# A linear-attention layer and an MLP on one core: transposing DMAs joined two by two, two more groups transposed by DMA, and w_in issued at the start

## The chip, the core and the metric

The kernel runs on one core of one Trainium2 chip, in one launch. The metric is the device time of that launch in microseconds (us), as the median of several runs; lower is better. Engines are named as the profile names them: PE (TensorE matmul; PEld is its weight load), DVE (VectorE), ACT (ScalarE), POOL (GpSimd), SP (the engine that here only issues DMAs). "SPq" is SP's queue.

## The reference, cut to what matters

Four batches, eight heads, 768 time steps, head size 48. Each head carries a 48 x 48 state that decays by w and takes in the outer product of k and v; the output of a step also takes the current outer product weighted by u. The result, as 3072 tokens of 384 numbers, goes through an MLP with 2048 hidden units and a smooth ReLU. Inputs and output are float32.

```python
for t in range(S):
    cur = einsum('bhd,bhe->bhde', u[None] * kt, vt)
    y[:, :, t] = einsum('bhd,bhde->bhe', rt, state + cur)
    state = w[None, :, :, None] * state + einsum('bhd,bhe->bhde', kt, vt)
x = y.transpose(0, 2, 1, 3).reshape(B * S, H * D)
h = x @ w_in
g = where(h >= 1, h, where(h <= -1, 0, (h + 1) ** 2 / 4))
out = g @ w_out
```

## The kernel before, in words

Time is cut into 6 chunks of 128 steps. A unit is one batch in one chunk; a group is two units (256 tokens). There are 12 groups, 0 to 11; groups 0 and 1 are the first chunk of the four batches, 2 and 3 the second, and so on.

For each group, the rows of R, K and V are loaded by SP (L364, L438; 384 KB each; group 0's R and K come in halves, one a unit). V is cast to bf16 by ACT (L248, tile V from VF). Then come four products over the whole group: Rs = R times powers of the decay (Wup, L383), Ks = K times inverse powers (Wdn, L385), KU = K times u (L387), RKU = R times KU (L389). In groups 0 to 2 each product is given to POOL or DVE, later ones are on POOL alone. DVE sums RKU over the head (diag, L411), and diag times V is the current step's term (V2, shown as tile V, L416).

For each unit, R and K must be turned so that the head dimension lies on the partitions. In groups 0 to 4 (`g < TDMA`) PE does it: 8 transposes (T, L462), copied to SBUF by ACT or DVE (TT, L248). In groups 5 to 11 SP issues two transposing DMAs a group (RT from Rs, KT from Ks, L546). Then PE computes A (L473), DVE masks it (AT, L478), PE computes the chunk's contribution to the state (Sp, L485) and the output Y (from the carried state L495, from AT L500), DVE adds V2 (y, L507). The state is updated by DVE (Tm, L515) and POOL (state, L520) and cast by ACT (state_bf). y is turned by PE in groups 0 to 2 (X, L528, copied as xT) and from group 3 on by a transposing DMA for each unit (xT, L569).

The MLP of a group runs in 4 steps q of 512 hidden units. Each step is 12 matmuls (hp, L602), relu(0.5 h + 0.5) (pt, L610) and its square (sq, L615) on ACT, and min and max on DVE (gt, L620). The second layer takes 4 matmuls a unit and step (op, L651; 32 a group); the result is copied (o_sb) and stored by SP (out, L666). Group 0's first layer is done in pieces of half a step and a unit at a time. Row tiles have 3 buffers for R, 3 for K and 2 for V in float32.

The weights are loaded by POOL's own DMAs with a cast to bf16: w_in in four parts (L320), w_out in four parts (L326). Ahead of the first part of each, POOL copies one number of a row tile (`gone`, L314), so that the DMA waits until that load has landed: R of group 0, unit 1, for w_in, and K of group 1 for w_out.

What sets the order: nothing is ordered by hand. Every step is entered as an operation with its engine or engines, a planned cost, a key and the steps that it needs. A planner at the end of the function takes, time after time, the operation of the smallest key among those that can start next on that engine, and writes it out. Each engine then runs its instructions in that order. The tables TUNE (added to the keys, by kind of operation and group) and ONLY (which engine, where there are two) come from a search. Where the planner sees PE idle in the early part, it fills in matmuls on an identity (warm, L679), whose result nobody uses.

SP, too, issues in this order: a transposing DMA that waits for Ks or y holds back every load and store behind it.

Of the kernel before, what the change touches and what calls it, by code (L numbers as in the profile page):

```python
# [15 lines left out]
P = 128  # L16
# [7 lines left out]
def kernel(  # L24
# [86 lines left out]
    Rs = [const.tile([P, UNITS * H, HP], BF16, name="Rs", tag=f"Rs{i}") for i in range(NB)]  # L111
    Ks = [const.tile([P, UNITS * H, HP], BF16, name="Ks", tag=f"Ks{i}") for i in range(NB)]
    for i in range(NB):
        nc.vector.memset(Rs[i][:, :, D:], 0.0)
        nc.vector.memset(Ks[i][:, :, D:], 0.0)
# [31 lines left out]
    FLEX, XDMA, TDMA, VCAST = 3, 3, 5, 12  # L147

    def shift(what, g):
# [17 lines left out]
        'Wdn': {0: -9.14},  # L167
        'Wup': {0: 1.93},
        'X': {0: 0.79, 1: -2.24, 2: -4.04},
        'Y': {0: -0.05, 3: 3.62, 10: 0.23, 11: -1.39, 'm': -2.74},  # L170
        'decay': {2: 0.48, 3: -11.42, 'm': -2.78},
        'exps': {0: 7.52},
        'gate': {0: 20.08, 1: 8.66, 2: -1.81, 3: -14.22, 10: 0.46, 'm': -3.69},
        'load': {0: -2.22, 1: 2.92, 2: 1.11, 11: 5.77, 'm': 11.7},
        'lw': {0: 3.06},
        'lw_row': {0: -3.75},
# [6 lines left out]
        'u_bc': {0: 6.26},  # L183
        'u_row': {'m': -2.41},
        'usum': {0: -0.67, 1: 19.78, 2: 1.23, 3: -1.67, 10: -0.52, 11: 1.53, 'm': -1.65},
        'wCm': {0: 9.26},
        'w_in': {0: -0.2, 1: -1.68, 2: -0.05, 3: 2.64},
        'w_in!': {0: -5.6, 1: 36.74, 2: 2.76, 3: -7.13},
        'w_out': {0: 0.06, 1: -8.78, 2: 4.51, 3: -1.32},
        'w_out!': {1: -0.28, 2: -2.83, 3: 4.56},  # L190
        'w_power': {0: 0.75},
        'w_row': {0: 3.3},
        'w_take': {0: 5.37},
        'wc': {0: 5.72},
        'xT': {0: 9.53, 1: -3.07, 2: 0.34, 3: -1.67, 10: 0.36, 11: 5.32, 'm': -2.7},
        'y': {0: -3.24, 1: 0.72, 2: 1.77, 3: -1.94, 10: -14.8, 11: 4.13, 'm': -3.61},
    }
    ONLY = {
        'KU': {2: 1},
        'Ks': {0: 1, 1: 1},  # L200
        'RKU': {1: 0},
        'Rs': {0: 0},
        'TT': {0: 0, 1: 0, 2: 1},
        'V2': {0: 0, 1: 0, 2: 0},
        'o': {0: 0, 1: 1, 2: 0, 3: 0},
        'xT': {0: 0, 1: 0, 2: 0},
# [87 lines left out]
    op("w_row", (("NET", 0.0, 3.4),), -99, None)  # L294
    op("u_row4", (("NET", 0.0, 4.4),), -99, None)
    op("lw_row", (("ACT", 0.52, 0.05),), -98, lw_ln, ["w_row"])
    op("lw", (("PE", 1.3, 0.17),), -98, lw_mm, ["lw_row"], [("bank", "lw")], ["lw"])
    op("wc", (("PE", 0.6, 0.17),), -99, w_mm, ["w_row"], [("bank", "wc")], ["wc"])
# [4 lines left out]
    op("w_take", (("DVE", 0.15, 0.08),), -95, w_take, ["wc"], [], ["wc"])  # L303
# [5 lines left out]
    GATE_IN = {0: ("R", 0, 1)}  # L309
    GATE_OUT = {0: ("K", 1, 1)}  # L310
    for i in range(max(NW, NO)):
# [25 lines left out]
        op(f"w_in{i}!", (("POOL", 0.78 + 0.2 * (i in GATE_IN), 1.5),), k_in, w_in_go, after(GATE_IN, i, "w_in"), [], [GATE_IN[i][:2]] if i in GATE_IN else [])  # L337
        op(f"w_in{i}", (("SWD", 2.5, 1.35),), k_in, None, [f"w_in{i}!"])
        op(f"w_out{i}!", (("POOL", 0.78 + 0.2 * (i in GATE_OUT), 1.5),), k_out, w_out_go, after(GATE_OUT, i, "w_out"), [], [GATE_OUT[i][:2]] if i in GATE_OUT else [])
        op(f"w_out{i}", (("SWD", 10.6 / NO, 1.35),), k_out, None, [f"w_out{i}!"])  # L340

    def turned(n, i, p):
        g, j = divmod(n, UNITS)
# [461 lines left out]
```

## Time and profile before

| What | Value |
|---|---|
| median of 3 runs | 183.79 us (183.52 to 184.97) |
| the profiled execution | 183.7 us |
| its span, first to last instruction | 181.9 us |
| busy: PE, DVE, ACT, POOL | 171.7, 140.2, 133.8, 111.6 us |
| filler matmuls (L679) | 182, busy 14.6 us |
| transposing DMAs | 18 xT, 7 RT, 7 KT |
| DMA traffic | 27.75 MB, mean 153 GB/s |
| first relu (group 0) | at 18.77 us |
| first w_in DMA, first w_out DMA issued | at 6.34 and 20.26 us |

How to read it: the page lists busy times, slices of the span, DMA queues, the chain of work that ended last and the costliest groups of instructions. Times of the chain and of the timeline count from the start of the span. A line of a group reads: line, engine, operation, output<-input, shape, count, busy us and mean ns, idle time ahead of it and what ended that. The pattern "x4" is a count. GB/s counts the bytes as written, so a weight that is cast on the way counts half of what is read.

### The profile page before, as it was taken

The numbers are of one execution on the slowest core, as the hardware profiler recorded it, in microseconds if no ns is written. First come the engines' busy times: TensorE is split into PE (matmuls) and PEld (weight loads), VectorE is DVE, ScalarE is ACT, GpSimd is POOL, SyncE is SP. The second block draws the span as 40 slices with busy tenths as digits, with TensorE's granted clock in tenths as the row PEclk, the third lists the DMA queues.
The fourth block names the chain that finished last, engine by engine and source line by source line (L and its number), as shares of the span: only waits on it lengthen the run. The fifth ranks groups of instructions, "written<-read, shape, count | busy, mean of one in ns | idle before, by whom it ended". The sixth has DMA issues, their size and how long they took to land.

```text
span 181.9 us, 4539 instructions
## 1 busy us (share of the span) xinstructions
PE 171.7 (94%) x1850; PEld 129.7 (71%) x1850; DVE 140.2 (77%) x207; ACT 133.8 (74%) x169; POOL 111.6 (61%) x88
## 2 busy tenths in 40 slices
PE   5999999969999999999998999999899999999992
PEld 4897888747778787587876677767667777777761
DVE  6977499599998879789986888768687998754360
ACT  5455896678767978668986987786977798774762
POOL 2793553029999998979939949898859551000000
PEclk9999999999999999999999999999999999999999
DMA  6999999999997599998989999889798822101032
GB/s 123 189 214 188 212 199 186 176 208 182 193 192 162 96 218 196 141 215 180 147 151 168 178 200 183 162 179 206 142 183 108 193 83 65 22 4 43 0 130 86
DMA packets 103806, 27.75 MB, mean 153 GB/s; under 512 B 97125, under 2 KB 103786, under 8 KB 103786
## 3 DMA queue, kind: packets, MB, share of 16 engines
q1 hardware_dynamic: 100064, 24.32, 75.5%
q0 software_dynamic: 3712, 3.15, 10.7%
q8 instruction: 14, 0.23, 0.6%
q14 instruction: 6, 0.05, 0.1%
q10 hardware_dynamic: 10, 0.01, 0.0%
HBM read 20.45 MB, written 4.72 MB: 138 GB/s over the span
## 4 chain that ended last, share of the span: by engine, by line
PE 41%; DMA 17%; POOL 14%; SPq 13%; DVE 7%; issue 3%; ACT 3%; DVEq 0%; ACTq 0%; POOLq 0%
PE op L651 18%; PE hp L602 17%; DMA K<-in_k_dram 14%; SPq L364 8%; POOL RKU L389 4%; POOL state L520 3%; DVE gt L620 3%; POOL Ks L385 3%; SPq L438 3%; POOL KU L387 3%; DMA R<-in_r_dram 3%; PE A L473 2%; ACT sq L615 2%; SPq L546 1%; PE T L462 1%
## 5 line engine op out<-in xcount | busy, mean ns | idle before, releaser
L620 DVE SCALAR_TENSOR_TENSOR gt<-sq,hp 128x1024 bf16<-128x1024 f32 (+1 forms) x52 | 58.7, 1134 | 25.5 <-ACT sq L615 25.1
L602 PE MATMUL hp<-xT,w_in_sb 128*128 128x256 bf16 (+1 forms) x624 | 71.7, 264 | 1.8 <-DVE gt L620 1.0
L651 PE MATMUL op<-w_out_sb,gt 128*128 128x384 bf16 x384 | 72.3, 326 | 0.1
L602 PEld LDWEIGHTS <-w_in_sb 128*128 128x128 bf16 x624 | 57.1, 98 | 14.1 <-issue 3.4
L610 ACT ACTIVATE pt<-hp 128x1024 f32<-128x1024 f32 (+1 forms) x52 | 49.6, 954 | 23.5 <-PE hp L602 23.4
L615 ACT ACTIVATE sq<-pt 128x1024 f32<-128x1024 f32 (+1 forms) x52 | 51.6, 992 | 1.1
L651 PEld LDWEIGHTS <-gt 128*128 128x128 bf16 x384 | 34.6, 97 | 18.7 <-DVE gt L620 0.4
L478 DVE TENSOR_TENSOR AT<-A,umask 128x512 bf16<-128x512 f32 x48 | 30.9, 682 | 3.7 <-PE A L473 3.7
L416 POOL TENSOR_TENSOR V<-V,diag 128x768 f32<-128x768 bf16 (+1 forms) x13 | 17.9, 1378 | 16.9 <-DVE diag L411 13.7
L383 POOL TENSOR_TENSOR Rs<-R,Wup 128x768 bf16<-128x768 f32 (+1 forms) x12 | 20.4, 1702 | 5.3 <-DMA R<-in_r_dram 5.0
L520 POOL TENSOR_TENSOR state<-Tm,wCm 128x384 f32<-128x384 f32 x16 | 16.0, 1004 | 5.3 <-DVE Tm L515 5.1
L389 POOL TENSOR_TENSOR RKU<-R,KU 128x768 f32<-128x768 f32 x10 | 18.1, 1819 | 1.4 <-DVE KU L387 1.2
L385 POOL TENSOR_TENSOR Ks<-K,Wdn 128x768 bf16<-128x768 f32 x9 | 16.4, 1825 | 0.9 <-PE hp L602 0.5
L387 POOL TENSOR_TENSOR KU<-K,u_bc 128x768 f32<-128x768 f32 x9 | 16.4, 1828 | 0.0
L679 PE MATMUL warm<-ident 128*128 128x128 bf16 x182 | 14.6, 242 | 1.5 <-POOL ident masks.py:199 1.5
L679 PEld LDWEIGHTS <-ident 128*128 128x128 bf16 x182 | 12.8, 110 | 2.8 <-POOL ident masks.py:199 1.5
L507 DVE TENSOR_TENSOR y<-Y,V 128x384 bf16<-128x384 f32 x24 | 13.1, 551 | 0.8 <-issue 0.2
L248 ACT CAST state_bf<-state 128x384 bf16<-128x384 f32 x20 | 9.8, 506 | 5.1 <-POOL state L520 3.9
L500 PE MATMUL Y<-V,AT 128*128 128x48 bf16 x192 | 11.4, 183 | 1.1 <-ACT V L248 0.9
L248 ACT CAST V<-VF 128x768 bf16<-128x768 f32 x12 | 9.9, 828 | 3.2 <-DMA VF<-in_v_dram 3.1
L411 DVE TENSOR_REDUCE diag<-RKU 128x16 f32<-128x768 f32 (+1 forms) x13 | 11.3, 881 | 1.0 <-POOL RKU L389 1.0
L248 ACT COPY o_sb<-op 128x384 f32<-128x384 f32 x16 | 7.6, 474 | 5.8 <-PE op L651 5.8
(63 smaller groups left out, 127.4 us busy)
## 6 DMA issues: line engine op xcount, KB each, us to landing
VF<-in_v_dram SPq DMA_DIRECT2D x12, 384.0 KB, 5.5
out_dram<-o_sb SPq DMA_DIRECT2D x24, 192.0 KB, 2.3
R<-in_r_dram SPq DMA_DIRECT2D x11, 384.0 KB, 4.6
K<-in_k_dram SPq DMA_DIRECT2D x11, 384.0 KB, 6.0
w_in_sb<-in_moe_w_in_dram POOLq DMA_DIRECT2D x4, 384.0 KB, 9.3
w_out_sb<-in_moe_w_out_dram POOLq DMA_DIRECT2D x4, 384.0 KB, 9.2
R<-in_r_dram SPq DMA_DIRECT2D x2, 192.0 KB, 3.4
K<-in_k_dram SPq DMA_DIRECT2D x2, 192.0 KB, 3.8
```

The source lines that it names most:

```text
L248: nc.scalar.copy(out, in_) if e == "ACT" else engines[e].tensor_copy(out, in_)
L385: engines[e].tensor_mul(part(K_s)[:, :, :, :D], part(K), rep(Wdn, j1 - j0))
L387: engines[e].tensor_mul(part(tiles["KU", g]), part(K), rep(u_row, j1 - j0))
L389: engines[e].tensor_mul(part(tiles["RKU", g]), part(R), part(tiles["KU", g]))
L478: nc.vector.tensor_mul(tiles["AT", n][:, i], tiles["A", n][i], umask.unsqueeze(1).to_broadcast([P, NP, P]))
L520: nc.gpsimd.tensor_mul(states[b], tiles.pop(("Tm", n)), wCm)
L602: nc.tensor.matmul(hp[:, f - f0, cols], w_in_sb[:, i, n0 : n0 + P], tiles["xT", g][:, i, cols], start=(i == 0), stop=(i == nK - 1), skip_g ...
L610: nc.scalar.activation(tiles["pt", g, q][:, f0:f1], tiles["hp", g, q, x], AF.Relu, bias=0.5, scale=0.5)
L615: nc.scalar.activation(tiles["sq", g, q][:, f0:f1], tiles["pt", g, q][:, f0:f1], AF.Square, bias=0.0)
L620: nc.vector.scalar_tensor_tensor(out=tiles["gt", g, q][:, f0:f1], in0=tiles["sq", g, q][:, f0:f1], scalar=1.0, in1=tiles["hp", g, q, x], o ...
L651: nc.tensor.matmul(tiles["op", g, j], tiles["gt", g, q][:, f, j * P : (j + 1) * P], w_out_sb[:, n, :], start=(n == 0), stop=(n == nF - 1),)
L679: nc.tensor.matmul(tiles["warm"][:, :P], ident, ident, start=True, stop=True, skip_group_check=True)
```

## The change

- The two tiles Rs and Ks become one, RKs. From group 3 on (`TDMA` is 3 instead of 5) one transposing DMA a group turns both R and K of both units (RKT, 16 blocks of 128 x 128 instead of two times 8). Groups 3 and 4 thus lose their PE transposes (4 units) and the TT copies.
- y of both units lies in one tile, and from group 3 on one transposing DMA turns both (xT, 6 blocks instead of two times 3). xT is laid out by unit, then by block.
- `GATE_IN` is empty: POOL issues w_in without waiting for a row load. In the order that comes out, three parts come right behind the mask, the fourth behind the seven small products of w_power, which are now on POOL.
- Planned costs of some operations are changed, and with them and new TUNE and ONLY tables the planner writes out another order on all engines. In it, group 0's KU and RKU are on POOL and its Rs and Ks on DVE; group 1's Rs, Ks and KU are on DVE and its RKU on POOL; group 2's Rs, KU and Ks are on POOL (Rs, KU, Ks were on DVE) and its RKU and V2 on DVE. The last part of w_out is issued behind Rs of group 2. The filler matmuls become 141, of which 63 stand between A of group 0 and its Sp and Y.

The diff, cut to its core (line numbers in the program's list above are those of the kernel before):

```diff
-    Rs = [const.tile([P, UNITS * H, HP], BF16, name="Rs", tag=f"Rs{i}") for i in range(NB)]
-    Ks = [const.tile([P, UNITS * H, HP], BF16, name="Ks", tag=f"Ks{i}") for i in range(NB)]
+    RKs = [const.tile([P, 2, UNITS * H, HP], BF16, name="RKs", tag=f"RKs{i}") for i in range(NB)]
...
-    FLEX, XDMA, TDMA, VCAST = 3, 3, 5, 12
+    FLEX, XDMA, TDMA, VCAST = 3, 3, 3, 12
...
     ONLY = {
-        'KU': {2: 1},
-        'Ks': {0: 1, 1: 1},
-        'RKU': {1: 0},
-        'Rs': {0: 0},
-        'TT': {0: 0, 1: 0, 2: 1},
-        'V2': {0: 0, 1: 0, 2: 0},
+        'KU': {0: 0, 2: 0},
+        'Ks': {2: 0},
+        'RKU': {0: 0, 1: 0, 2: 1},
+        'Rs': {2: 0},
+        'TT': {1: 0, 2: 1},
+        'V2': {0: 0, 1: 0},
...
-    GATE_IN = {0: ("R", 0, 1)}
+    GATE_IN = {}
...
-                y = tiles["y", n] = att.tile([P, DM], BF16, name="y", tag="y", bufs=3)
+                if j == 0:
+                    tiles["y", g] = att.tile([P, UNITS, DM], BF16, name="y", tag="y", bufs=2)
...
-                    for i in range(2):
-                        def t_dma(e, g=g, i=i):
-                            t = tiles["RK"[i] + "T", g] = att.tile([P, UNITS * NP, P], BF16, name="RK"[i] + "T", tag="RK"[i] + "T", bufs=2)
-                            nc.sync.dma_start_transpose(out=t, in_=tiles["scaled", g][i].rearrange("p h d -> p (h d)"))
...
-                        op(f"{'RK'[i]}T{g}", (("DMA", 1.4, 3.0),), ka - 2 + i, t_dma, [f"{w_}{part}"] + ([f"RT{g}"] if i else []),
+                    def t_dma(e, g=g):
+                        t = tiles["RKT", g] = att.tile([P, 2 * UNITS * NP, P], BF16, name="RKT", tag="RKT", bufs=2)
+                        nc.sync.dma_start_transpose(out=t, in_=RKs[g % NB].rearrange("p i h d -> p (i h d)"))
+
+                    op(f"RKT{g}", (("DMA", 1.9, 2.7),), ka - 1.5, t_dma, [f"Rs{part}", f"Ks{part}"],
+                       [("RKT", ("RKT", g))], [("RKT", g), ("Rs", g), ("Ks", g)])
...
-                nc.sync.dma_start_transpose(out=tiles["xT", g][:, :, j * P : (j + 1) * P], in_=tiles["y", n])
+                tiles["xT", g] = moe.tile([P, UNITS, nK, P], BF16, name="xT", tag="xT", bufs=3)
+                nc.sync.dma_start_transpose(
+                    out=tiles["xT", g].rearrange("p u k t -> p (u k) t"), in_=tiles["y", g].rearrange("p u c -> p (u c)")
+                )
...
-                op(f"xT{n}", (("DMA", 1.2, 2.0),), ka + 3, x_dma, [f"y{n}"], [] if j else [("xT", ("xT", g))], [("y", n), ("xT", g)])
+            elif j == UNITS - 1:
+                op(f"xT{n}", (("DMA", 1.36, 1.6),), ka + 3, x_dma, [f"y{n - y}" for y in range(UNITS)], [("xT", ("xT", g))], [("y", g), ("xT", g)])
...
-                fill(int((spare - 0.1) / (0.11 if s < 7 else 0.06)))
+                fill(int((spare - 0.25) / (0.1 if s < 10 else 0.075)))
```

The tables TUNE, most planned costs and the times at which the planner lets each engine begin are changed as well and not shown.

More of the change, by code (lines that the diff above doesn't have):

```diff
@@ L185 @@
[L185 to L195, printed above, removed]
@@ new lines @@
+        'lw': {0: 1.04},
+        'lw_row': {0: -1.56},
[8 rows of a table added]
+        'wCm': {0: 0.97},
+        'w_in': {0: -1.94, 1: 0.83, 2: 1.91},
+        'w_in!': {0: 1.1, 1: 9.21, 2: 2.99, 3: 0.5},
+        'w_out': {0: -0.94, 1: -13.99, 2: -2.85, 3: -0.92},
+        'w_out!': {0: -1.21, 1: -0.54, 2: 2.86, 3: 1.24},
+        'w_power': {0: 1.68},
+        'w_row': {0: 7.69},
+        'w_take': {0: -1.25},
+        'wc': {0: 3.84},
+        'xT': {0: -2.42, 1: -3.58, 2: -3.06, 3: -4.14, 10: -0.73, 11: -6.46, 'm': -1.35},
@@ L207 @@
+        'o': {0: 0, 1: 1, 10: 1, 11: 0},
+        'w_power': {0: 0},
+        'xT': {2: 1},
     }
@@ L336 @@
         k_out = -1 + i * 0.1 + shift("w_out", i)
[L337 to L340, printed above, removed]
+        op(f"w_in{i}!", (("POOL", 0.78 + 0.6 * (i in GATE_IN), 2.5),), k_in, w_in_go, after(GATE_IN, i, "w_in"), [], [GATE_IN[i][:2]] if i in GATE_IN else [])
+        op(f"w_in{i}", (("SWD", 2.5, 0.6),), k_in, None, [f"w_in{i}!"])
+        op(f"w_out{i}!", (("POOL", 0.78 + 0.5 * (i in GATE_OUT), 2.5),), k_out, w_out_go, after(GATE_OUT, i, "w_out"), [], [GATE_OUT[i][:2]] if i in GATE_OUT else [])
+        op(f"w_out{i}", (("SWD", 10.6 / NO, 0.6),), k_out, None, [f"w_out{i}!"])
     def turned(n, i, p):
@@ L669 @@
             op(f"o {o}", where, k2 + 0.2 + shift("o", g), o_out, [f"mm2 {o}{nQ - 1}"], [("o_sb", ("o_sb", o))], [("op", o), ("o_sb", o)])
-            op(f"out {o}", (("DMA", 0.45, 2.0),), k2 + 0.3, store, [f"o {o}"], [], [("o_sb", o)])
+            op(f"out {o}", (("DMA", 0.62, 2.0),), k2 + 0.3, store, [f"o {o}"], [], [("o_sb", o)])
     WARM = (2.2, 99.0)
@@ L704 @@
     left = dict(users)
-    free = {"POOL": 3.9, "DVE": 3.0, "DMA": 1.55}
+    free = {"POOL": 2.2, "DVE": 3.0, "DMA": 0.7, "ACT": 3.2}
     done = {}
```

76 lines of the change are left out of this document (32 added, 44 removed), and 40 rows, old and new, of the table TUNE.

## The prediction

> **What bounds the kernel now.** I read four views in this order: the page's first parts, busy time by stretches, the chain of waits in order of time, and the timeline with the DMA landings of the first 40 us.
>
> Busy time by stretches (columns: stretch, its length, then busy us of PE, PEld, DVE, ACT, POOL, the granted clock, DMA share, GB/s):
>
> ```profile
> 0.00:38.60 38.60, 34.21 (x468) 28.82 (x469) 29.40 (x64) 25.73 (x40) 16.96 (x26) 1.00 1.20 188
> 38.60:178.60 140.00, 137.47 (x1382) 100.84 (x1382) 110.79 (x144) 107.56 (x128) 94.67 (x62) 1.00 0.79 144
> 40.00:80.00 40.00, 39.97 (x440) 29.58 (x439) 34.74 (x48) 30.33 (x38) 37.94 (x24) 1.00 1.04 176
> 80.00:140.00 60.00, 57.51 (x602) 42.74 (x599) 49.30 (x66) 48.54 (x60) 49.55 (x34) 1.00 0.95 169
> ```
>
> From 38.6 to 178.6 us TensorE pauses for only 140.00 - 137.47 = 2.5 us, all of it between 80 and 140 us. So the end is where that stretch begins, plus the matmul work left, plus 2.5 us. Before 38.6 us, busy PE means little: 182 matmuls there are filler (warm, L679).
>
> The chain of waits shows what opens the stretch: group 2's K lands late and its products follow.
>
> ```profile
> 19.69 16.02 DMA K<-in_k_dram
> 35.73 0.97 DVE KU L387
> 36.72 0.96 DVE RKU L389
> 37.68 0.88 DVE Ks L385
> 38.60 0.40 PE T L462 x4
> ...
> 45.75 0.45 PE T L462 x8
> ```
>
> The timeline gives the prices for the start:
>
> ```profile
> 6.34 0.93 POOL L320 DMA_DIRECT2D w_in_sb<-in_moe_w_in_dram  x1
> 8.98 0.83 ACT L248 CAST V<-VF 128x768 bf16<-128x768 f32 x1 [1.85 <-DMA VF<-in_v_dram]
> 16.60 0.56 DVE L507 TENSOR_TENSOR y<-Y,V 128x384 bf16<-128x384 f32 x1
> 18.77 0.60 ACT L610 ACTIVATE pt<-hp 128x512 f32<-128x512 f32 x1 [0.58 <-PE hp L602]
> 19.39 0.63 ACT L615 ACTIVATE sq<-pt 128x512 f32<-128x512 f32 x1
> ```
>
> The DMA landings (count, median us from issue to landing):
>
> ```profile
> xT<-y SPq DMA_TRANSPOSE x18, 2.4
> RT<-Rs SPq DMA_TRANSPOSE x7, 3.7
> KT<-Ks SPq DMA_TRANSPOSE x7, 4.1
> ```
>
> The page's traffic by slices of 4.55 us:
>
> ```profile
> GB/s 123 189 214 188 212 199 186 176 208 182 193 192 162 96 218 196 141 215 180 147 151 168 178 200 183 162 179 206 142 183 108 193 83 65 22 4 43 0 130 86
> ```
>
> After the first slice it is flat near 195 up to slice 11 (55 us), with row loads alone or with weights beside them. So there, bytes set the landings.
>
> **The change part by part**, against the profiled execution: 183.7 us, a span of 181.9 and 1.8 around it. The median of the runs is 183.79, so the two agree within 0.1.
>
> *1. Groups 3 and 4 lose their PE transposes.* Four units, each 8 transposes at 0.45 us (45.75 row): 4 x 0.45 = 1.8 us. They lie in 40 to 80 us, where PE is busy 39.97 of 40, so all of it counts: -1.8. Four TT copies (0.68 on DVE, 0.99 on ACT) go too; neither engine bounds there, so I count nothing.
>
> *2. w_in at the start.* In the new order GpSimd issues three parts right after umask (ends at 1.98), and the fourth after the seven w_power products moved onto it (1.34 on DVE before). What arrives late is group 0's row data. w_in's first part was issued at 6.34, yet R of group 1 landed at 10.96 (issued 4.36, 6.6 to landing), just 2.06 after V of group 0 (8.9), as if alone: the stream started about 3.9 us after its issue. Issued at 2.0 it starts near 6. By then rows have moved (6.2 - 2.05) x 0.2 = 0.83 of group 0's 1.18 MB: R and K are in, V's 0.35 MB is not. While w_in's parts landed (12.4 to 21.9) rows got about 45 to 60 of 195 GB/s. V lands between 12.8 (60 GB/s from the first moment: 6.2 + 0.35/0.06 + 0.8 to land) and 17.0 (all rows wait for all of w_in: 2.75 MB at 0.195, from 2.05, plus 0.8). I take 15.1, just over what 45 GB/s gives (14.8), the nearer row because w_in's first part came at almost full rate. Before it was 8.9. The other things moved onto GpSimd ahead of that are hidden by this wait: w_power done near 6.6 (5.3 before), KU and RKU of group 0 (4 x 0.92) near 11.
>
> *3. From V to the first MLP.* Cast 0.84: 15.95. V2 of both units is on GpSimd, 0.81 each, so the second y starts 1.7 later, at 17.65. From that y's start to the first relu the trace shows 18.77 - 16.60 = 2.17. First relu: 19.8, which is 1.0 later than before. The 63 fillers queued ahead of Sp take 63 x 0.061 = 3.8 us (29 took 1.78), from about 10.3, so they end by then. Filler ahead of the first transposes falls from 58 to 22.
>
> *4. From there to group 2.* ACT now runs in order six relu/square pairs (0.58 + 0.63 = 1.21 each, 7.3), two TT (1.9) and V of group 1 (0.84): 29.85. Then GpSimd: V2 of group 1 (1.47), KU (1.83), Ks (1.83) of group 2, which were 0.96 each on DVE: 35.0. K of group 2 must land by 31.3; before, it waited behind all four w_out parts (35.7). Now the last part of w_out is issued only after Rs of group 2, and by bytes K lands at 29 to 32. So the first transpose of group 2 comes near 35.0, against 38.60 with half of it already done (0.22). But before had by then also done 24 matmuls of group 1's first layer, 2.62 us, which now come after. Gain: 38.60 - 35.0 - 2.62 - 0.22 = 0.8; I take 0.7. V's bounds move it one to one: from +2.7 (V at 12.8, cut by K of group 1) to -1.2 (17.0).
>
> *5. Joined transposes.* 3 blocks land 2.3 us after issue and 8 blocks 3.2 at best: (3.2 - 2.3)/5 = 0.18 a block. By that line 16 blocks (R and K) need 4.7 and 6 (both units of x) 2.9. The bounds for 16 are 4.2 (no dearer than a lone KT) and 8.0 (two in sequence, 3.7 + 4.3 at the slower medians); I take 4.9. A pair cost two issues of 1.25 on SP and then 4.1, or 5.4, so A waits no longer where both were late. What is queued behind: SP works in order, and a joined transpose waits for Ks, with the next K, V and R behind it. Group 3 is the tight one. Its R lands about 38, Rs 1.82, state 1.0, Ks 1.83 on GpSimd: 42.8; behind an output store, issued at 44; landed about 49.8 with R of group 4 ahead on the queue. PE gets there 14.8 us of work after 35.0, at 49.8: level. I charge 0.5 (bounds 0 and 3.4, the last by 8.0 at issue to landing). For xT, y of both units must be in before one transpose of 2.9, where the second one alone took 2.4: 0.5 later. At group 3 the new order has 16 op matmuls, one hp set, A and Sp between, 4.6 us, against 0.55 (y) + 2.9: covered.
>
> *6. More bytes.* Two groups more by DMA: 2 x 2 x 0.262 = 1.05 MB, 5.4 us at 195 GB/s. Between 40 and 140 us the DMA moved 17.2 MB; at 195 to 200 it could move 19.5 to 20, so it fits in 2.3 MB or more of gaps: 0. If the order closes the gaps the price is up to 5.4.
>
> *7. The end.* 28 op matmuls follow the last hp, 20 of them ahead of what waits for the last gate: 20 x 0.163 = 3.26 against 1.02 + 1.06 + 1.21 + hops = 3.4. Before there were 32. +0.2.
>
> Sum: -1.8 - 0.7 + 0.5 + 0 + 0.2 = -1.8, so 183.7 - 1.8 = 181.9 us.
>
> One rule weighed. The trace puts 3.9 us between w_in's issue and its effect on other traffic. The Trainium skill, "DMA: Bandwidth & Descriptors", Specifications, gives about 1 us to the first byte on the GpSimd path. By it the stream would start near 3.8 instead of 6, more of the rows would lie behind it, V would come at 16.1 to 17.0, and the sum would be 182.9 to 183.8. The same page (Issuing engines are not separate DMA queues) says an earlier start on another queue saves issue time only, which speaks against part 2, and the flat 185 to 195 GB/s agrees. I keep the row, because R of group 1 was measured unslowed.
>
> **The rivals.**
>
> *A. PE waits for joined transposes.* A sixteen-block transpose needs 7 us or more, so A of group 3 waits 2 us and xT of a group once more. For it: part 5 has no slack at group 3. Against: later groups have 2 to 3 us, since GpSimd needs 4 x 1.82 + 1.47 + 2.0 = 10.8 a group and PE about 12.3. Time: 181.9 + 1.8 = 183.7, no change.
>
> *B. The DMA becomes the bound (slower).* Place: groups 3 to 6, 44 to 80 us. Rows, transposes and stores need about 2.3 MB a group, 11.8 us at 195 GB/s against 12.3 of PE. It decides when SP, waiting for Ks or y, leaves more than 0.5 us a group empty until the lead is gone; then the 5.4 us reach PE in full. For it: in the stretch 62 to 63 us the trace shows 6 GB/s, with SP waiting. Against: 32 transposing issues become 18. Time: 181.9 - 0.5 + 5.4 = 186.8.
>
> *C. More than forecast.* V lands at 13, and the 2.5 us of PE idle time at 80 to 140 shrink because K and V are issued sooner. Time: 181.9 - 1.4 - 1.0 = 179.5. For it: SP's 14 fewer issues; against: nothing shows that those waits were for SP's issue time.
>
> **How the numbers follow.** Forecast 0.48 (own range 180.3 to 183.2 by parts 2 and 5), A 0.20, B 0.17, C 0.15. The range 179.6 to 186.2 leaves out about half of B and half of C, under 2 in 10. One per cent, 1.84 us, is about what a measurement of this kernel can tell from no change: the limits are 181.95 and 185.6. Under the lower one lie a little over half of the forecast's chance and C: 0.43. Within: the rest of it, A and a little of B: 0.38. Over: most of B and a mishap at the start: 0.19.
>
> **What would show it.** Right: V's cast near 16, first relu near 19.8, the first T of group 2 near 35, no T after it beyond group 2, A of group 3 near 50 with a wait under 1 us, PE idle after 36 us under 4 us. Wrong: V at 9 or K of group 2 after 32 (parts 2 and 4), a joined transpose over 6 us from issue to landing (part 5, A), PE waiting repeatedly for A or for K rows from 50 to 90 us with GB/s near 195 throughout (B).

## The result and the profile after

The changed kernel takes 185.24 us in the median (183.61 to 187.02, 20 runs) against 183.46 us (182.13 to 184.97, 20 runs): 1.009 times as long, 95% interval 1.0062 to 1.0117. I forecast 181.9 us. All ratios here leave out disturbed runs, those over 1.5% above the fastest of their kernel, so they can differ from the quotient of two medians, which is 1.004 for e8, 1.009 for e9, 1.011 for e10 and 0.994 for e14.

The first profiled execution took 183.61 us, the fastest of the 20. A second one (run e8, another chip) took 186.36 us, 0.5 us above the median of its own 12 runs. Both are needed: the median of the 20 lies between them.

Busy time by stretches, first execution; the stretches begin and end with the first T of group 2 and PE's end, as in the prediction. The first records of the granted clock begin at 17.78 us in this execution and at 21.46 in the second; a 1.00 in the clock's column ahead of them stands for no record.

```profile
0.00:38.30 38.30, 29.94 (x400) 24.61 (x401) 24.75 (x50) 21.91 (x37) 23.59 (x36) 1.00 1.18 188
38.30:178.10 139.80, 138.38 (x1379) 101.04 (x1377) 113.26 (x147) 109.78 (x127) 93.47 (x62) 1.00 0.80 152
40.00:80.00 40.00, 38.86 (x417) 27.99 (x415) 36.12 (x51) 31.50 (x37) 34.78 (x23) 1.00 1.06 182
80.00:140.00 60.00, 60.00 (x619) 44.74 (x617) 51.73 (x70) 51.67 (x62) 56.84 (x39) 1.00 1.03 197
```

The stretch that I had called full is even fuller: PE pauses 139.80 - 138.38 = 1.4 us, not 2.5. What I forecast wrongly lies ahead of it. The timeline of the same execution:

```profile
13.16 1.37 POOL L384 TENSOR_TENSOR KU<-K,u_bc 128x384 f32<-128x384 f32 x1 [4.72 <-DMA K<-in_k_dram]
13.73 0.61 PE L459 MATMUL T<-ident,RKs 128*128 128x128 bf16 x4 [2.66 <-DVE RKs L382]
15.89 4.57 PE L677 MATMUL warm<-ident 128*128 128x128 bf16 x63
17.21 0.83 ACT L245 CAST V<-VF 128x768 bf16<-128x768 f32 x1 [6.16 <-DMA VF<-in_v_dram]
...
20.30 0.50 PE L482 MATMUL Sp<-V,RKs 128*128 128x96 bf16 x8
...
23.93 0.60 ACT L608 ACTIVATE pt<-hp 128x512 f32<-128x512 f32 x1 [0.38 <-PE hp L600]
...
38.29 0.76 PE L459 MATMUL T<-ident,RKs 128*128 128x128 bf16 x8
```

K of group 0's second unit lands at 13.1, V at 17.2 (8.9 before), and the 63 fillers, queued behind A of that unit, hold PE until 20.46, though V was cast by 18.04. The first relu starts at 23.93 (18.77 before), the first T of group 2 at 38.29. The same lines in the second execution:

```profile
15.93 1.37 POOL L384 TENSOR_TENSOR KU<-K,u_bc 128x384 f32<-128x384 f32 x1 [7.48 <-DMA K<-in_k_dram]
...
18.16 0.83 ACT L245 CAST V<-VF 128x768 bf16<-128x768 f32 x1 [6.03 <-DMA VF<-in_v_dram]
18.66 5.01 PE L677 MATMUL warm<-ident 128*128 128x128 bf16 x63
...
23.51 0.50 PE L482 MATMUL Sp<-V,RKs 128*128 128x96 bf16 x8
...
27.14 0.60 ACT L608 ACTIVATE pt<-hp 128x512 f32<-128x512 f32 x1 [0.38 <-PE hp L600]
...
41.50 0.76 PE L459 MATMUL T<-ident,RKs 128*128 128x128 bf16 x8
```

K lands 2.8 us later, V 0.95, Sp starts 3.2 later, and so does all that follows: from the first relu to the first T of group 2 it is 14.36 us in both, from the first Sp to PE's end 157.8 and 157.4.

The clock at the start differs too. The same transposes, and fillers, in before:

```profile
9.82 0.39 PE L462 MATMUL T<-ident,Rs 128*128 128x128 bf16 x4
10.26 1.78 PE L679 MATMUL warm<-ident 128*128 128x128 bf16 x29
```

Four transposes take 0.39 us there and 0.61 at 13.73 above. In all these traces the matmuls of such a row start 106 to 107 ns apart at first, and 55 to 56 ns from the first record of the granted clock on. That is at 9.08 us in before, 17.78 in the first execution after and 21.46 in the second: until then the changed kernel ran at half clock.

The DMA landings (median us from issue) and the page's traffic by slices, first execution:

```profile
RKT<-RKs SPq DMA_TRANSPOSE x9, 5.9
xT<-y SPq DMA_TRANSPOSE x9, 3.5
```

```profile
GB/s 111 196 191 210 185 194 209 198 179 119 147 192 180 195 227 154 246 211 224 207 193 183 226 167 209 226 214 215 215 139 132 4 45 87 44 90 0 49 42 87
```

For the balance I took all real matmuls (all but warm) from the trace, merged their intervals, and counted PE's other time by stretch. Work + other = PE's end, on a clock that starts 0.25 us ahead of the profile's:

```
execution       work   other: 0-20  20-46  46-end   PE's end
before          159.8        11.25   5.22    2.52      178.8
after, first    158.3        13.92   5.10    0.98      178.3
after, second   158.1        13.91   7.93    1.15      181.1
```

So the change saves 1.5 to 1.7 us of work and 1.4 to 1.5 us of pauses behind 46 us, and loses 2.6 to 5.4 us up to 46 us: -0.5 in the lucky execution, +2.3 in the second.

### The profile page after: what moved, and what is told of

The parts are those of the page before. It is cut to its first block, busy times and chain, and to the rows that moved or that the text cites. A ratio compares the mean times of both kernels' runs of the same rounds, so it can differ in the third digit from the quotient of the medians.

```text
span 181.7 us, 4338 instructions
## 1 busy us (share of the span) xinstructions
PE 168.3 (93%) x1777; PEld 125.6 (69%) x1777; DVE 138.0 (76%) x196; ACT 132.1 (73%) x163; POOL 117.1 (64%) x97
## 4 chain that ended last, share of the span: by engine, by line
PE 73%; DMA 11%; DVE 10%; ACT 2%; issue 2%; SPq 1%; DVEq 0%
PE hp L600 31%; PE op L649 28%; DMA K<-in_k_dram 6%; DMA xT<-y 5%; PE A L470 4%; PE warm L677 3%; PE Y L497 2%; DVE gt L618 2%; PE Y L492 2%; PE Sp L482 2%; DVE diag L408 2%; DVE AT L475 1%; DVE y L505 1%; ACT sq L613 1%; SPq L361 1%
## 5 line engine op out<-in xcount | busy, mean ns | idle before, releaser
L649 PE MATMUL op<-w_out_sb,gt 128*128 128x384 bf16 x384 | 73.4, 326 | 0.2 <-DVE gt L618 0.2
L618 DVE SCALAR_TENSOR_TENSOR gt<-sq,hp 128x1024 bf16<-128x1024 f32 (+1 forms) x52 | 58.6, 1133 | 18.4 <-ACT sq L613 18.1
L608 ACT ACTIVATE pt<-hp 128x1024 f32<-128x1024 f32 (+1 forms) x52 | 49.7, 956 | 22.4 <-PE hp L600 21.9
L384 POOL TENSOR_TENSOR KU<-K,u_bc 128x768 f32<-128x768 f32 (+1 forms) x12 | 20.7, 1723 | 4.7 <-DMA K<-in_k_dram 4.7
L386 POOL TENSOR_TENSOR RKU<-R,KU 128x768 f32<-128x768 f32 (+1 forms) x12 | 20.1, 1680 | 4.9 <-DVE KU L384 4.2
L382 POOL TENSOR_TENSOR RKs<-K,Wdn 128x768 bf16<-128x768 f32 x10 | 18.2, 1820 | 2.6 <-DMA K<-in_k_dram 2.5
L413 POOL TENSOR_TENSOR V<-V,diag 128x768 f32<-128x768 bf16 (+1 forms) x12 | 16.4, 1368 | 4.7 <-ACT V L245 2.3
L380 POOL TENSOR_TENSOR RKs<-R,Wup 128x768 bf16<-128x768 f32 x10 | 18.2, 1821 | 1.4 <-DMA R<-in_r_dram 1.3
L518 POOL TENSOR_TENSOR state<-Tm,wCm 128x384 f32<-128x384 f32 x16 | 15.9, 1004 | 2.6 <-DVE Tm L513 2.6
L505 DVE TENSOR_TENSOR y<-Y,V 128x384 bf16<-128x384 f32 x24 | 13.1, 553 | 2.9 <-POOL V L413 2.2
L677 PE MATMUL warm<-ident 128*128 128x128 bf16 x141 | 12.1, 252 | 1.5 <-POOL ident masks.py:199 1.5
L677 PEld LDWEIGHTS <-ident 128*128 128x128 bf16 x141 | 10.4, 115 | 3.0 <-POOL ident masks.py:199 1.5
L497 PEld LDWEIGHTS <-AT 128*128 128x128 bf16 x192 | 9.5, 96 | 0.7
```

Of the source, the lines that this page charges most:

```text
L380: engines[e].tensor_mul(part(R_s)[:, :, :, :D], part(R), rep(Wup, j1 - j0))
L384: engines[e].tensor_mul(part(tiles["KU", g]), part(K), rep(u_row, j1 - j0))
L386: engines[e].tensor_mul(part(tiles["RKU", g]), part(R), part(tiles["KU", g]))
L497: nc.tensor.matmul(Y[:, 2 * p + i, :], AT[:, i, p, :], V[:, j * H + 2 * p + i, :], start=(c == 0), stop=True, skip_group_check=True,)
L608: nc.scalar.activation(tiles["pt", g, q][:, f0:f1], tiles["hp", g, q, x], AF.Relu, bias=0.5, scale=0.5)
L618: nc.vector.scalar_tensor_tensor(out=tiles["gt", g, q][:, f0:f1], in0=tiles["sq", g, q][:, f0:f1], scalar=1.0, in1=tiles["hp", g, q, x], o ...
```

## The experiments

So that an edit moves only what it names, each kernel has the order of work of its parent written out as a list of (operation, engine, fillers ahead of it). Two units of a group share the group's name. "Before" is the kernel before, run beside each on the same chip.

**Where is the loss: at the start or in the transposes? (e1 to e4)**

e1, the changed kernel with fewer fillers:

```diff
-('Sp0', 'PE', 63)
+('Sp0', 'PE', 20)
```

> The changed kernel in its own order, with 20 instead of 63 filler matmuls between A and Sp of group 0; nothing else. Theory S (start): the change lost its time before 39 us, because V of group 0 lands at 17.1 instead of 8.9 and the fillers then hold PE until 20.3 although V is cast at 18.0. By S the first relu comes 2.2 us earlier (21.7 instead of 23.9), the first transpose of group 2 near 36.1 instead of 38.3, and the time falls by 1.5 to 2.2 us against the changed kernel, to 183.0 to 183.7, about the kernel before. Theory J (joined transposes): the loss is in the middle, where PE waits for xT at 62 to 66 and 75 to 79 us; those waits grow by what the start gives, and the time stays within 0.5 us of the changed kernel, 184.7 to 185.3.

Measured: 185.03 us, ratio 1.0075 (1.004 to 1.0109). In the profiled execution K landed at 15.2, V at 17.8, and Sp began at 20.14, still 1.5 us behind the cast of V, since the 20 fillers ran at half clock and took 2.32 us. Beside e8, where 63 fillers hold Sp until 23.51, that is 3.4 us earlier; from there to PE's end it took 159.2 us instead of 157.4, and in the medians no more than 0.2 to 0.8 us of it is seen. The time is in theory J's range: PE's pauses behind 46 us are 2.0 us against e8's 1.15, and the real matmuls take 159.2 us against 158.1, which neither theory has. The fillers make the loss larger, they are not all of it: with K at 15.2 and V at 17.8 the start stays late.

e2, the changed kernel with w_in gated again (first two parts behind w_power, the others behind RKU of unit 1, 6 fillers ahead of Sp):

```diff
-    GATE_IN = {}
+    GATE_IN = {0: ("R", 0, 1)}
```

> The changed kernel in its own order, but w_in waits again for R of group 0, unit 1 (w_power ahead of it; its third and fourth part behind KU and RKU of group 0; 6 fillers instead of 63 ahead of Sp). All the rest, joined transposes and groups 3 and 4 by DMA, as changed. Theory S: V lands near 9, the first relu comes at 18 to 19.5 instead of 23.9, the first transpose of group 2 at 34 to 36.5, limited by what the DMA has moved by then, and the time falls by 2 to 4 us against the changed kernel: 181.3 to 183.3, faster than the kernel before by 0 to 2. Theory J: the gain is taken back by the waits for xT and RKT in the middle: 184 to 185.

Measured: 186.03 us, ratio 1.0175 (1.0133 to 1.0217). The first relu is back near 19, and PE's other time up to 46 us is back at before's 16.5 us (19.0 to 21.8 in the changed kernel): that loss comes with the early w_in and its fillers (6 here). Yet the time is above both theories' ranges: work is 160.3 us, other time behind 46 us 3.2, and the first T of group 2 stays at 38. One wait that holds T back is in the timeline:

```profile
27.83 0.81 ACT L245 CAST V<-VF 128x768 bf16<-128x768 f32 x1
30.07 1.81 POOL L380 TENSOR_TENSOR RKs<-R,Wup 128x768 bf16<-128x768 f32 x1 [4.61 <-DMA R<-in_r_dram]
31.84 0.80 POOL L323 DMA_DIRECT2D w_out_sb<-in_moe_w_out_dram  x1
32.66 1.49 POOL L413 TENSOR_TENSOR V<-V,diag 128x768 f32<-128x768 bf16 x1
...
34.80 0.96 PE L526 MATMUL X<-ident,y 128*128 128x128 bf16 x6 [2.89 <-DVE y L505]
```

V2 of group 1 could start at 28.6, but on GpSimd it stands behind Rs of group 2, which waits 4.61 us for R. The new order fits rows that come late; with early rows it waits elsewhere.

e3, before's order with w_in's four parts issued right behind the mask, no gate:

```diff
-    GATE_IN = {0: ("R", 0, 1)}
+    GATE_IN = {}
```

> The kernel before in its own order, with one part of the change alone: w_in's four parts issued right behind the mask, waiting for no row load. Theory S: V of group 0 lands at about 17 instead of 8.9, the first relu comes at 22 to 24 instead of 18.8, and the time rises by 2 to 4 us, to 185.5 to 187.5. Theory J: the start is hidden by the load of group 2 that comes late in both, so the time changes by less than 1 us: 182.7 to 184.4.

Measured: 190.49 us, ratio 1.0414 (1.038 to 1.0448). V is cast at 18.25, PE stands 8.06 us ahead of A (behind the cast on ScalarE stands the copy of T), the granted clock falls to 0.50 from 15.8 to 26.0 us, the first relu starts at 28.67. This is the early w_in alone, in an order that is not made for it: +7 us, more than S had (2 to 4).

e4, the changed kernel with each joined transpose issued as two at the same place:

```diff
-nc.sync.dma_start_transpose(out=t, in_=RKs[g % NB]...)
+for i in range(2):
+    nc.sync.dma_start_transpose(out=t[:, i * UNITS * NP : (i + 1) * UNITS * NP], in_=RKs[g % NB][:, i]...)
```

> The changed kernel in its own order, but each joined transposing DMA is issued as two in the same place (R, then K; unit 0, then unit 1, both still after both y). Theory S: the joining is not where the loss lies; one more issue of about 1.2 us for each of 18 transposes makes SP later and the waits for xT a little longer: 185 to 186.5. Theory J: the big transposes are what comes late; split, the first halves land sooner and the loads behind mix in, and the time falls to 183.5 to 184.7.

Measured: 191.69 us, ratio 1.0441 (1.0398 to 1.0484), far above S's range, with 6.8 us of PE's other time behind 46 us against 1.0 to 1.15, in a profiled execution of 193.89 us, 2.2 above the median. In this order the joining is worth some 6 us; it is not the loss.

**The parts of the change in before's order, and the bytes (e5 to e7)**

e5, before's order, joined transposes only (for groups 3 on, `xT` of the first unit and `RT` dropped from the list, `KT` becomes `RKT`).

> The kernel before, in its own order of work, with one edit: the transposing DMAs are joined (one for R and K of a group, one for both units' y). Groups 3 and 4 are still turned by PE, and w_in is gated as before. Theory S (the loss is made in the first 46 us, where PE's time without real matmuls went from 16.5 us to 19.0): the start is as before (first relu 19.0, first T of group 2 at 37.0), and joining moves the time by no more than 0.7 us either way: 182.6 to 184.0 beside 183.3. Theory J (the joined transposes make PE wait in the middle, as the 4.2 to 6.3 us from issue to landing in the changed kernel suggest): PE's time without real matmuls after 46 us grows from 2.5 us to 4 or more, and the time is 185 or above.

Measured: 183.44 us, ratio 0.9988 (0.9963 to 1.0013): level, as S had it. So the 6 us of e4 are what two issues cost in an order planned for one, not a gain of joining over before.

e6, as e5 and groups 3 and 4 by DMA:

```diff
-('T6', 'PE', 0) ... ('TT9', 'DVE', 0)
+('RKT3', 'DMA', 0)   behind 'load R4.0'
+('RKT4', 'DMA', 0)   behind 'out (1, 0)'
```

> As the run before (before's order, joined transposing DMAs, w_in gated) and also groups 3 and 4 turned by DMA: their eight PE transposes and copies out of PSUM are gone, the joined transpose of group 3 is issued behind the load of R of group 4, that of group 4 behind the first store of group 1, and the first A of group 3 moved to just ahead of the second. This is the whole change without its new start. Theory S: PE has 1.5 us less real work (158.3 us instead of 159.8, as the changed kernel showed), some of it lost to a wait for the first A of group 3; 181.5 to 183.2, that is faster than both kernels or level with before. Theory J: A of group 3 and the xT that come late cost more than the 1.5 us: 184.5 or above.

Measured: 186.41 us, ratio 1.0141 (1.0116 to 1.0166). Slower, against S and in J's range. Work fell to 159.0, but other time behind 46 us rose to 5.4. The timeline:

```profile
57.00 2.68 SPq L543 DMA_TRANSPOSE RKT<-RKs  x1
59.77 0.53 SPq L435 DMA_DIRECT2D VF<-in_v_dram  x1
...
63.86 0.83 ACT L245 CAST V<-VF 128x768 bf16<-128x768 f32 x1 [2.48 <-DMA VF<-in_v_dram]
...
66.73 1.22 DVE L618 SCALAR_TENSOR_TENSOR gt<-sq,hp 128x1024 bf16<-128x1024 f32 x1 [3.11 <-ACT sq L613]
```

My place for RKT4 held back V of group 5 on SP (issued at 54.89 in before, 59.77 here), ScalarE waited for it, and a gate came late (1.83 us on PE); around A of group 3 PE paused 1.57 us besides. The first is a loss by place, not by the transpose itself.

e7, the changed kernel without the last two parts of w_out (the second layer reads the first two twice):

```diff
-w_out_sb[:, n, :]
+w_out_sb[:, n % (nF // 2), :]
```

> The changed kernel in its own order, but the last two of w_out's four parts are not loaded, and the second matrix product reads the first two parts twice: 0.79 MB less come in before R and K of group 2, and the output is not the reference's. Theory D (what limits the start is the bytes: the 16 DMA engines are busy from 6 to 36 us at 190 to 205 GB/s, and R and K of group 2 lie behind 6.3 MB, so that no order of the weights brings them earlier): first T of group 2 comes about 0.79 MB / 0.19 MB per us = 4.1 us earlier, at 34.5 to 36 instead of 38.5, PE's time without real matmuls from 20 to 46 us falls from 5.1 us to 2 to 4, and the time falls to 182.5 to 184.3. Rival L (the late first V, at 17 us, and what the engines then do one after the other set the start): first T of group 2 stays within 1 us of 38.5, and the time stays at 184.5 to 185.7.

Measured: 185.56 us, ratio 1.0088 (1.0058 to 1.0118). First T of group 2 at 40.78, not earlier. Theory D fell: the bytes ahead of group 2 don't set its T in the changed kernel. The time is in L's range. K of unit 1 landed at 14.4 here and Sp began at 22.79, which puts T later than L had it; again 158.0 us from Sp to PE's end.

**Second profile, and the two groups in the new order (e8, e10)**

e8 is the changed kernel unaltered.

> The changed kernel once more, unaltered, for a second profiled execution: the first one was the fastest of 20, 1.6 us under the median. Theory C (the time follows the landing of the first V and of K of group 0's second unit, which lie behind the stream of w_in, by a fixed chain: first Sp to end of PE took 157.8 us in the changed kernel's profile, 158.1 with half of w_out, 159.2 with 20 fillers): in this execution that K lands at 14.5 to 15.5 us instead of 13.1, V is cast at 17.5 to 18.3, Sp starts at 22 to 23 instead of 20.5, first T of group 2 at 40 to 41 instead of 38.5; time 185 to 185.6. Theory M (the start is the same in every execution, and the spread comes from the middle): Sp at 20.5 and T at 38.5 again, with more of PE's time without real matmuls after 46 us than the 1.0 us of the first profile.

Measured: 185.85 us, ratio 1.013 (1.0091 to 1.0168). Before beside it has a median of 185.15. Theory C holds in its mechanism: 157.4 us again from first Sp to PE's end, and 1.15 us of other time behind 46 us, so M falls. Of C's numbers only the cast of V (18.16) lies in its range; K at 15.9, Sp at 23.51, T at 41.50 and the time are all a little later than said.

e10, the changed kernel with groups 3 and 4 by PE:

```diff
-('RKT3', 'DMA', 0), ('RKT4', 'DMA', 0)
+('T6', 'PE', 0), ('TT6', 'DVE', 0) ... ('T9', 'PE', 0), ('TT9', 'DVE', 0)
```

> The changed kernel in its own order, with groups 3 and 4 turned by PE as before: the two joined transposes of those groups are gone, four T of 8 matmuls and their copies by DVE are put in ahead of A of those units. What the part with the two groups gains in the changed kernel's own order: if it gains the 1.5 us of PE work that the counts show, this kernel is 1 to 2 us slower than the changed one (186 to 187.2). If the gain is eaten by the wait for the joined transposes and by SP's 4 us at its issue, it is level (184.8 to 185.8). If the part costs, as in before's order (2.9 us there), it is faster than 184.5.

Measured: 187.24 us in the median of five runs, ratio 1.0164 (1.0082 to 1.0247); a sixth took 593 us and is left aside (with it the median is 187.57). Against e8 the intervals overlap. The counts of the two profiled executions say it more sharply: 159.7 us of work against 158.1, and 159.4 us from first Sp to PE's end against 157.4. By them the two groups by DMA gain 1.6 to 2.0 us in the new order.

**Can the gated order be mended? (e9, e12 to e14, and e11)**

e9, e2 with V2 of group 1 ahead of Rs of group 2, and Ks ahead of w_out's last part and KU, all on GpSimd:

```diff
-Rs2.0, w_out3!, V21.0, KU2.0, Ks2.0
+V21.0, Rs2.0, Ks2.0, w_out3!, KU2.0
```

> The kernel with w_in gated again in the changed kernel's order (first relu at 19.3, yet 186.0 us) and one more edit: on GpSimd, V2 of group 1 goes ahead of Rs of group 2, and Ks of group 2 ahead of the last part of w_out and of KU. In the run without this edit Rs of group 2 waited for R until 30.07, and V2 of group 1, ready at 29, stood behind it until 32.66; the X of group 1 waited 2.89 us on PE for it. Theory G (GpSimd's order, written for rows that come early, took back what the earlier first relu had given): the wait of 2.9 us at X goes, first T of group 2 comes at 34 to 36 instead of 38.4, and the time falls by 2 to 4 us to 182 to 184. Rival X (the transfers set the middle whatever the start does): T comes earlier and PE waits as much more for the joined transposes after 46 us (3.2 us before the edit, 5 or more after): 185.3 or above.

Measured: 186.84 us, ratio 1.0135 (1.0061 to 1.021). The time is rival X's, the place is not: first T of group 2 came 4.9 us earlier than in e2, PE's other time behind 46 us is 3.5 us where X had 5 or more, and a new wait took the gain back:

```profile
PE A L470 <- DVE TT L245: 4.1, 1, 4.1
PE hp L600 <- DMA xT<-y: 2.4, 2, 1.6
```

The copy of T stood on VectorE behind RKU of group 2, which now waited for KU.

e12, e9 with that mended on VectorE:

```diff
-RKU2.0, TT4, usum2.0, V22.0, AT4.0, AT4.1
+TT4, AT4.0, AT4.1, RKU2.0, usum2.0, V22.0
```

> The gated kernel with GpSimd's order mended, and the wait mended that came in its place. There first T of group 2 came at 33.4 as meant, but PE stood 4.07 us ahead of A of group 2: the copy of T on DVE lay behind RKU of group 2, which waited 4.92 us for KU, now later on GpSimd. Here the copy of T and the two products of A go ahead of RKU, the sum and V2 of group 2 on DVE. Theory G: the 4.1 us at A become 0 to 1, hp of group 2 starts 3 us earlier than there, 54.8 to 52, and the time falls from 186.8 by 2.5 to 4 us to 183 to 184.3. Rival X (the joined transposes in the middle take it back: PE waited 2.5 us at xT there): the time stays above 185.3.

Measured: 187.15 us (183.73 to 188.48, 6 runs). The run with a mean granted clock of 1.0 took 183.73, in G's range; the five with 0.96 to 0.99 took 186.7 to 188.5. The profiled one, by stretches (the granted clock is the third number from the end):

```profile
8.00:10.00 2.00, 0.72 (x13) 0.62 (x12) 2.00 (x2) 0.18 (x1) 2.00 (x2) 1.00 1.44 191
10.00:12.00 2.00, 1.68 (x27) 1.07 (x25) 1.51 (x3) 1.66 (x2) 2.00 (x3) 0.85 1.23 193
12.00:14.00 2.00, 1.97 (x22) 1.53 (x19) 2.00 (x5) 0.00 (x0) 1.98 (x4) 0.50 1.21 192
14.00:18.00 4.00, 3.33 (x40) 3.06 (x40) 3.82 (x7) 1.73 (x4) 1.58 (x2) 0.50 1.24 213
```

and its waits, where the next one is seen:

```profile
PE op L649 <- DMA w_out_sb<-in_moe_w_out_dram: 3.1, 1, 3.1
PE hp L600 <- DMA xT<-y: 2.0, 3, 1.1
```

e13, e12 with more fillers early (the number is that ahead of the operation):

```diff
-wc 2, T0 20, A0 0, A1 4, Sp0 6, Y0 0, X0 6, X1 3, mm1 (0, 1)10 10
+wc 8, T0 44, A0 6, A1 8, Sp0 8, Y0 8, X0 8, X1 5, mm1 (0, 1)10 16
```

> The last gated kernel with more fillers on PE in the first 20 us and nothing else: 8 instead of 2 ahead of the first small product, 44 instead of 20 ahead of the first T, 8 instead of 4 to 6 ahead of A, Sp, Y and X, 16 instead of 10 in mm1. There PE had no work from 8.1 to 9.4 us and a granted clock of 0.50 from 12 to 18 us; it had 161.1 us of real matmuls in place of 158.3. Theory W (the gated order loses about 2 to 3 us to the clock alone): granted clock 1.0 from 2 to 36 us, real matmuls 158 to 159.5 us, and the time falls from 186.7 to 188.5 down to 183.5 to 185. Rival X (the lower clock is made up by waits that follow): the time stays above 185.5.

Measured: 183.22 us (182.63 to 184.62), ratio 1.0007 (0.9976 to 1.0038). Every one of its 12 runs is below the five of e12 at a lower clock, but the one run of e12 at a clock of 1.0 lies among them. So what the fillers are worth is shown only against runs at a lower clock, and one run at 1.0 is too few to settle it. By stretches:

```profile
10.00:20.00 10.00, 8.96 (x153) 7.86 (x151) 7.44 (x13) 4.60 (x8) 7.86 (x10) 1.00 1.23 201
20.00:36.00 16.00, 13.36 (x195) 10.67 (x193) 11.90 (x19) 13.19 (x23) 8.24 (x7) 1.00 1.19 198
36.00:46.00 10.00, 7.85 (x72) 5.61 (x69) 7.97 (x10) 4.57 (x6) 6.37 (x5) 0.83 0.83 140
46.00:140.00 94.00, 93.08 (x968) 68.49 (x967) 81.81 (x111) 78.09 (x93) 87.42 (x58) 1.00 1.07 196
```

The clock of 10 to 20 us is 1.00 (0.66 in e12), work 159.2 us instead of 161.1, and of PE's other time behind 46 us 1.1 is left instead of 3.1. The fillers also moved the first Sp back, 13.0 to 13.7, and it cost nothing that can be seen.

e14, e13 with w_out's last part issued ahead of Rs of group 2:

```diff
-V21.0, Rs2.0, Ks2.0, w_out3!, KU2.0
+V21.0, w_out3!, Rs2.0, Ks2.0, KU2.0
```

> The same with the fillers, and the last quarter of w_out issued on GpSimd ahead of Rs of group 2 instead of behind Ks. In the kernel before, it was issued at 35 and PE stood 3.10 us at 39.5 for it, 1.06 of xT later on. Theory O (with the four waits named one after the other mended - V2 behind Rs, the copy of T behind RKU, the clock, this part of w_out - the gated start is worth its 5 us less what R and K of group 2 lose to the weights): the 3.1 us at the second product become under 1, and the time is 181.3 to 183.3, below before. Rival X (PE then waits at A of group 2, or for joined transposes in the middle): 183.8 or above.

Measured: 182.26 us (180.35 to 184.62), ratio 0.9902 (0.9861 to 0.9942), quotient of the medians 0.994: 0.6 to 1% faster than before, and by the comparisons with before 1.5 to 2% faster than the changed kernel, beside which it was not run. The wait for w_out is gone. Theory O holds in its main point; a new wait of 2.0 us for a gate at 42 us and a clock of 0.89 from 36 to 46 us are left:

```profile
PE hp L600 <- DVE gt L618: 3.4, 5, 2.0
PE T L459 <- POOL RKs L382: 1.4, 1, 1.4
```

e11, before's order with joined transposes and group 4 alone by DMA, its transpose behind the load of V of group 5:

```diff
-('T8', 'PE', 0), ('TT8', 'DVE', 0), ('T9', 'PE', 0), ('TT9', 'DVE', 0)
+('RKT4', 'DMA', 0)   behind 'loadV5'
```

> Before's order with joined transposes (level with before when run alone) and group 4 alone turned by DMA, its joined transpose issued behind the load of V of group 5. In the run with groups 3 and 4, 2.9 us were lost, of which the trace shows two causes: A of group 3 stood 1.57 us on PE because its transpose could not be issued before Ks was written at 44.6; and the transpose of group 4 stood ahead of the load of V of group 5 on SP, which went out at 59.8 instead of 54.9, so that ScalarE's cast waited and a gate came 3.1 us late (1.83 us on PE). Theory P (place on SP and lead time decide what a group by DMA is worth): without these two waits the 0.75 us of PE work for one group is gained: 182.3 to 183.4. Rival J (transposes by DMA cost more than they save in this order wherever they stand): 184.5 or above.

Measured: 184.01 us, ratio 1.0014 (0.9972 to 1.0056). Whether the 0.75 us are gained stays open: work is 159.4 us (160.1 in e5), but the issue took SP 3.88 us with xT of group 3 behind it. The 2.9 us of e6 are gone. The time lies between P's range and J's: group 4 costs nothing in a better place, but the gain that P had is not seen; group 3 was not tried in another place.

## Why the prediction was wrong, step by step

**Step 2 (w_in at the start) failed.** I had the stream start near 6 with "R and K are in, V's 0.35 MB is not". Its first packets went at 4.66 us (4.15 in the second execution); from 2 to 4.5 us the rows' queue had moved 0.48 of 1.18 MB, and K of unit 1 was not in. The traffic from 8 to 14 us in the first execution (queue 0 carries the weights, queue 1 the rows; packets, MB, share of the engines):

```profile
q0 software_dynamic: 966, 0.96, 93.9%
q1 hardware_dynamic: 968, 0.18, 27.7%
```

The rows got 0.18 MB in 6 us, 30 GB/s, where I had 45 to 60. Before's own trace shows 30 as well where both queues are full: from 13 to 19 us they moved 955 and 950 packets, and the rows 0.18 MB. The stretch that I had read, 12.4 to 21.9, takes in the time from 20 us on, in which the weights' queue is nearly empty (47 packets from 20 to 22). So K came at 13.1 to 15.9 and V at 17.2 to 18.1, at and above my upper bound of 17.0. The nearer end was the one at which all rows wait for all of w_in.

**Step 3 (V to the first MLP) failed on the fillers.** I had the 63 fillers run from 10.3 and end under V's wait. They stand behind T and A of unit 1, which wait for K; the late K shifted them to 15.89 and 18.66, and they reached 2.3 and 4.5 us past the cast of V. First relu at 23.93 and 27.14, not 19.8. With K mis-timed in step 2, what I had costed at nothing lost its cover. The fillers were also longer, 4.57 and 5.01 us instead of 3.8, because they began at half clock. I had noted that the fillers ahead of the first transposes fall from 58 to 22, and drawn nothing from it. Whether it is these fewer fillers that keep the clock low is argued, not shown: no run adds them with w_in early, and the share of the clock in the late start is not told apart.

**Step 4 was right in its length and wrong in its start.** From first relu to first T of group 2 I had 15.2 us; it is 14.36. But it starts 4.1 to 7.3 us late: 38.29 and 41.50 instead of 35.0, a loss in place of the gain of 0.7. That it is this and not the bytes of w_out, e7 shows.

**Step 1 was right:** 1.8 us forecast, 1.5 to 1.7 by the counts, 1.6 to 2.0 by e10.

**Step 5 was right in the sum, low in the durations.** 16 blocks land 5.9 us after issue in the median (4.9 forecast, bounds 4.2 to 8.0), 6 blocks 3.5 (2.9 forecast); for the two that PE waited for, the chain has 4.20 and 4.65:

```profile
61.71 4.20 DMA xT<-y
74.64 4.65 DMA xT<-y
```

PE waited 0.30 + 0.36 us there (0.5 charged). A of group 3 came at 54.12 and waited for nothing, since the late start had given its transpose time. SP's issue of one RKT takes 2.1 to 4.2 us, which I had not counted. In before's order (e5) the medians are 4.3 and 2.8 us and most issues 1.8 to 1.9, so part of the length comes with the new order.

**Step 6 was right:** 1.05 MB more go through (197 GB/s mean from 80 to 140 us) and PE pauses there not at all. **Step 7:** 0.21 us are seen at the end, as charged. What I had only in rival C is that PE's pauses behind 46 us shrink, by 1.4 us (C had 1.0, and with it an early V, which did not come). e5, with the transposes joined in before's order, doesn't show it (2.9 us there), so it belongs to the new order; how much of it is owed to loads that run ahead while PE stands at the start is not told apart.

None of the rivals names what happened at the start. I weighed a row against a page and kept the row. The Trainium skill, "DMA: Bandwidth & Descriptors", Specifications, with its 1 us to the first byte, led to V at 16.1 to 17.0 and to 182.9 to 183.8 us. The traces put the first weights 2.2 to 2.7 us after their issue (3.3 in before), so the page's figure is not what they show, and the later V has another cause: the rows' small share. Nor did the early start move more bytes: up to 38 us it is 7.15 MB before and 7.13 after, 3.94 and 3.96 of them by the rows' queue, so only their order changed. The slices there run from 176 to 214 GB/s, not from 185 to 195.

In the runs, then: with w_in early, late rows, fillers and half clock together cost 2.6 to 5.4 us at the start of the new order; the two groups by DMA give 1.6 to 2.0 back; joining is level in before's order. With the gate back and four faults behind it mended (two places in a queue, the clock, w_out's last part), the same order gains 0.6 to 1% on before (e14). Gating it without mending lost as much as it won (e2). What the gate alone gives in the mended order is open, since the mended order was not run without it.

## What to carry to other kernels

When a bulk transfer is moved ahead of small urgent loads, price the small ones by their share of the packets, and follow each of them to the first instruction behind it on an in-order engine: a filler, a cast or a gate there turns the delay into a longer one. An order tuned for late data must be mended wait by wait when data come early; one part put back tells little, since the next wait takes its place at once. Early fillers also hold the clock up (e13 against e12): when some are taken away, read the clock, from the spacing of the matmuls where the trace has no record of it. Profile a kernel twice when its runs spread by 2%: the first trace may be the luckiest.

## What the hardware showed that I had not expected

**Packets take turns one for one.** From 8 to 14 us the two queues moved 966 and 968 packets in the first execution of the changed kernel, 954 and 968 in the second, 963 and 951 in e1, 958 and 958 in e3; before moved 955 and 950 from 13 to 19 us. A packet of the rows carries 186 bytes, one of the weights 994, so the rows' share is 186 / (186 + 994) = 16%, which gives the 30 of 190 GB/s. The Trainium skill, "DMA: Bandwidth & Descriptors", Queues, rings and completion order, says that each engine goes round robin between the queues that have work, packet by packet; the trace agrees, with these counts. Had I used it, the forecast for V would have been my own upper bound, 17.0.

**The clock starts at half, and can fall again after a thin stretch.** In before and in e3, e5, e6 and e11, which keep its order, the matmuls' spacing goes from 106 or 107 to 55 or 56 ns at 9.0 to 10.4 us; in the changed kernel and in e1, e4, e7 and e10 at 17.8 to 22.8. So in e8 the pause of 4.35 us (12.1 to 16.5) fell into a time at half clock, and there was no full clock to lose. In e12's profile the clock was full from 8.00, PE was idle for 1.28 us (8.1 to 9.4) and sparsely used until 11.41, and the records show 0.50 from 11.41 to 18.24; in e3 8.06 us of idling were followed by 0.50. The records, but for the last of each run, last 3.41 us or a multiple of it (3.41, 6.83, 20.48, 23.89). The Trainium skill, "TensorE: Matmul & The Clock Gate", What's actually happening, has a free-running window of about 3.4 us behind it, so that the same kernel can differ between runs. The steps and the differing runs of e12 agree with that; a fall after 1.28 us does not follow from one idle window. How thin a step must be, the runs don't settle: in e9 one with PE busy 56% of the time is followed by a fall, one with 47% is not.

**Issuing a transpose is not cheap for SP.** In the changed kernel one RKT of 16 blocks holds SP for 2.1 to 4.2 us, one joined xT for 1.2 to 2.5, where a load at a quiet moment takes 0.4 to 0.5 and one at a full moment up to 8.5. In before a single RT, KT or xT holds it for 1.2 to 2.6.
